# A parallel attention and feed-forward block: where small stores, statistics, splits and side work stand in the queues

## The chip, the cores and the metric

The kernel runs on one core of a Trainium2 chip. A core has five engines with a queue each: TensorE (PE in the profile; its weight loads are shown as PEld), VectorE (DVE), ScalarE (ACT), GpSimd (POOL) and SyncE (SP), which here only issues transfers. The metric is the device time of one execution in microseconds (us), as the median of several runs. An engine works through its instructions in the order in which the program wrote them; engines wait for each other, and for transfers, by semaphores.

## The reference

For x of 2048 rows and 576 columns the reference computes

```
xn  = layernorm(x)                       # no scale, no shift, eps 1e-5
out = x + A(xn) + B(xn)

A:  q, k, v = xn @ wqkv, 32 heads of 18
    for row s: 8 keys at s, s-2, ..., s-14 (masked below 0)
    softmax over the 8 logits (scale 18**-0.5), weighted sum of v, @ wo
B:  h = relu(xn @ w1 + b1) ** 2          # 4608 columns
    h @ w2 + b2
```

All inputs are float32.

## The kernel before, in words

**Precision.** TensorE multiplies in a 32-bit form of reduced precision (fp32r). So every operand is split into a high part (a copy on ACT) and a low part (a subtraction on DVE), and a product is made of several matmuls: `split`, `wq_hi`/`wq_lo`, `w1_hi`/`w1_lo`, `w2_hi`/`w2_lo`, `normalize`. A split on ACT followed by one on DVE therefore stands ahead of every group of matmuls.

**Blocks and stages.** The 2048 rows are 4 blocks (`b`) of 512, and the columns of the features are 5 tiles of 128 (the last has 64). Heads are 4 groups (`g`) of 8. The program runs through these stages:

- `open_rows`: normalises block 0 row by row and multiplies group 0 of Q, K, V. The first inverse deviation is a `pow` on GpSimd (`inverse_std`, L130).
- `q0`: 28 rows of Q, K, V products (`qkv_row`, L301 to L306; a row is 14 matmuls of 432 columns) for blocks 0 and 1, of which 26 run in its loop and two in the first pair that follows. Between the rows generators in `pieces` are advanced: `statistics(1)`, the splits of the weights of a group (`split_wq`), `normalize(1)`, the sums of blocks (`sums`).
- `phase_a(0)`: 18 pairs (`ffn_pair`) of tiles of the hidden layer for blocks 0 and 1 together, by a scheme with fewer products out of sums of blocks and of W1's parts (`combine_w1`, slots T1 to T4). Block 0's second product (`tile_products`, L494) is interleaved as `work(0..3)`; block 1's hidden tiles go to DRAM (`hscr`).
- `phase_b0`: block 1's second product, tile by tile, from the hidden tiles loaded again, with the Q, K, V rows of blocks 2 and 3 between.
- `phase_a(1)` and `phase_b1`: the same for blocks 2 and 3. In each stage the attention output of a block is regrouped (`regroup`, from DRAM by GpSimd's queue), transposed on DVE (`o_hi`) and multiplied by wo (`o_ops`) at the end.

**Attention as side work.** Attention runs on DVE (`attention`, a generator of 18 steps for a block and group: 8 for the logits, 2 for the softmax, 8 for the weighted sum). `side(k)` advances it by k steps; with `exp=False` it stops ahead of the step that holds the exponential on ACT. `run(pieces, k)` advances the pieces first and gives what is left of k to `side`. `queue` holds the groups offered so far, `loads` and `fetch` their transfers, and three buffers `kv` limit how many are loaded. `complete(b)` finishes all of a block's attention at once.

**What sets the order.** The order is written out by hand; nothing is rearranged. Rows of Q, K, V are copied from PSUM into the one tile `st` (`qkv_out`, L295) and stored two rows at a time by SP (L298), so the copy of a row into one half of `st` comes after the landing of the stores that read this half. In `q0`, `turn_mr` transposes the statistics of block 1 on TensorE, copies and stores them, and `load_mb` loads them again for all partitions; `normalize(1)` needs that load. SP's transfers are issued in the order of the program, and each load waits on SP until its buffer is free. The keys' and values' scratch has 16 rows of zeros ahead of it: 8 small stores (`scr[k][g][:PAD]`), two by SP ahead of `open_rows` and six behind it.

**In a pair** (`ffn_pair`), PSUM banks `ba`, `bb`, `bc` hold the products. DVE adds `bc` and the copy `u` (`tt(r1[:, 1], ...)`, `tt(r0[:, 1], ...)`) between two products into the same bank, so TensorE waits for these sums. The first pair of a stage (`first`) has another order at its end (`fourth` ahead of `third`).

Of the kernel before, what the change touches and what calls it, by code (L numbers as in the profile page):

```python
# [25 lines left out]
G = 4  # L26
# [5 lines left out]
PAD = 16  # L32
# [13 lines left out]
def block_kernel(ctx: ExitStack, tc: tile.TileContext, x, xt, wqkv, wo, w1, b1, w2, b2, out):  # L46
    nc = tc.nc
# [19 lines left out]
    zero = sb.tile([PAD, CG], F32, name="pr")  # L67
# [437 lines left out]
    def ffn_pair(s, p, work, first=False):  # L505
        b0, b1 = 2 * s, 2 * s + 1
        n = s * NP + p
        ba, bb, bc = (bank(i) for i in F_BANKS[s])
        f0, f1 = 2 * p, 2 * p + 1
        last = p == NP - 1  # L510
        A11 = lambda k, c: X[b0][:, k, c]
        A12 = lambda k, c: X[b0][:, k, 2 + c]
        A22 = lambda k, c: X[b1][:, k, 2 + c]
        S4 = lambda k, c: X[b1][:, k, c]
        ss = lambda i: lambda k, c: SS[i][:, k, c]

        def weight(slot, k, c):
            return w1s[n, slot // 4][:, k, slot % 4, c * P:(c + 1) * P]

        def product(to, slot, a, start=False):  # L520
            mm = [(weight(slot, 0, c), a(0, c)) for c in range(2)]
            for c in range(2):
                mm += [(weight(slot, 1, c), a(0, c)), (weight(slot, 0, c), a(1, c))]
            for i, (l, r) in enumerate(mm):
                nc.tensor.matmul(to, l, r, start=start and i == 0, stop=i == len(mm) - 1, skip_group_check=True)  # L525

        def left(to, f, v):
            for k in range(2):
                nc.tensor.matmul(to, weight(LEFT, k, f), v, start=False, stop=k == 1, skip_group_check=True)  # L529

        def relu(to, a, f):
            nc.scalar.activation(to, a, AF.Relu, bias=b1t[:, f:f + 1])  # L532

        def square_hi(r):
            h = mt.tile([P, 2, 2, TB], F32R, name="h", bufs=3)
            nc.scalar.activation(h[:, 0], r, AF.Square)  # L536
            return h

        def square(r):
            nc.scalar.activation(r, r, AF.Square)  # L540

        def square_lo(r, h):
            tt(h[:, 1], r, h[:, 0].bitcast(F32), ALU.subtract)

        def finish_pair():
            r0, r1, h0 = prev.pop("r")
            h1 = square_hi(r1)
            square_lo(r0, h0)
            square(r1)
            yield  # L550
            square_lo(r1, h1)
            nc.sync.dma_start(hscr[s][p], h1.rearrange("p k f t -> p (k f t)").bitcast(F32))
            yield

        before = prev.pop("finish", None)
        product(ba, B11, A11, start=True)
        if first:
            nc.tensor.matmul(bb, weight(B11, 0, 0), A11(0, 0), start=True, stop=True, skip_group_check=True)
        nc.scalar.activation(bb, ba, AF.Copy)
        product(bc, T1, ss(1), start=True)  # L560
        if before:
            next(before)
        if not last:
            combine_w1(n + 1)
        if not first:
            side(1, False)
        work(0)
        product(bb, T2, ss(2))
        w2_hi()
        u = four()  # L570
        nc.scalar.activation(u[:, 0], bb, AF.Copy)
        if not first:
            left(bc, 1, x4[b1])
        work(1)
        if before:
            next(before)
        w2_lo()
        if not last:
            w1_hi(n + 1, 0)
        w2_hi()  # L580
        product(bb, T3, ss(3))
        if first:
            left(bc, 1, x4[b1])
        if not last:
            w1_lo(n + 1, 0)
        w2_lo()
        nc.scalar.activation(u[:, 1], bb, AF.Copy)
        r0, r1 = four(), four()
        tt(r1[:, 1], bc, u[:, 1], ALU.add)
        if not last:  # L590
            w1_hi(n + 1, 1)
            w1_lo(n + 1, 1)
        product(ba, B21, A12)
        left(ba, 0, x4[b0])
        relu(r1[:, 1], r1[:, 1], f1)
        relu(r0[:, 0], ba, f0)
        work(2)

        def third():
            product(bc, B22, S4)  # L600
            left(bc, 1, x4["d"])
            side(2)
            tt(r0[:, 1], bc, u[:, 0], ALU.add)
            relu(r0[:, 1], r0[:, 1], f1)

        def fourth():
            product(bb, T4, A22)
            left(bb, 0, x4[b1])
            relu(r1[:, 0], bb, f0)

        if first:
            fourth()
            third()
            h0 = square_hi(r0)
        else:
            third()
            h0 = square_hi(r0)
            fourth()
        square(r0)
        side(2, False)  # L620
        work(3)
        hs[n] = h0
        prev["r"] = r0, r1, h0
        prev["finish"] = finish_pair()
# [126 lines left out]
    def phase_b0():  # L751
# [8 lines left out]
        for n in range(NF):  # L760
            w2_hi()
            add(b, tile_products(b, n, hs[0, n // 2]))
            w2_lo()
            if n % 2 and n // 2 + 3 < NP:
                load_h(0, n // 2 + 3)
            run(pieces, 2 if n < 9 else 1)
            while r < 32 and 32 * (n - 6) > 25 * r:
                bb, g, j = todo[r]
                while bb not in normed or g not in split_up:
                    run(pieces, 1)  # L770
                qkv_row(bb, g, j, 2 + r % 3)
                r += 1
                if r == 2:
                    pieces.append(split_wq(1, "w1s", lambda: load_wq(2)))
                if r == 8:
                    pieces.append(split_wq(2, "S", lambda: load_wq(3)))
                if r == 16:
                    pieces.append(split_wq(3, "w1s"))
                if r == 24:
                    pieces.append(sums(1))  # L780
                if j == NJ - 1 and bb == 2:
                    offer(2, g)
                run(pieces, 2)
            if n == 31:
                run_all(pieces)
                last_sum(1)
                complete(1)
                load_w1(NP)
                load_w1(NP + 1)
                regroup(b, 0)  # L790
                regroup(b, 1)
                for g in range(G):
                    offer(3, g)
            if n == 33:
                residual(b)
                combine_w1(NP)
            if n in (33, 34):
                c = 2 * (n - 33)
                o_hi(b, c), o_hi(b, c + 1)
                o_lo(b, c), o_lo(b, c + 1)  # L800
# [26 lines left out]
    def phase_b1():  # L827
        b = 3
        open_y(b)
        for n in range(NF - 2):  # L830
            w2_hi()
            add(b, tile_products(b, n, hs[1, n // 2]))
            w2_lo()
            if n % 2 and n // 2 + 3 < NP:
                load_h(1, n // 2 + 3)
            if n == 22:
                complete(b)
                regroup(b, 0)
                residual(b)
                residual_left(b)  # L840
            if n == 25:
                regroup(b, 1)
            if n in range(27, 27 + NC):
                o_hi(b, n - 27)
                o_lo(b, n - 27)
            side(2)
        for c in range(NC):
            w2_hi()
            add(b, o_ops(b, c), (NC - 2,) if c == NC - 1 else ())
            w2_lo()  # L850
        tail()
# [213 lines left out]
    def q0():  # L1065
# [20 lines left out]

        for r in range(len(todo) - 2):
            row(r)
            if r == 2:
                run_all(pieces)  # L1090
                turn_mr(1, 7)
                load_mb(1)
                load_wq(2)
                offer(0, 0)
                for late in held:
                    late()
                held.clear()
                pieces += [normalize(1)]
            if r == 5:
                lane[0] = nc.gpsimd  # L1100
                load_w1(0)
                pieces.insert(0, split_wq(2, "h", lambda: load_wq(0)))
# [7 lines left out]
            if r == 21:  # L1110
                run_all(pieces)
                for n in range(3):
                    load_w2(n)
            if r == 23:
                combine_w1(0)
                load_w1(1)
            if r in (24, 25):
                w1_hi(0, r - 24)
                w1_lo(0, r - 24)
            elif r != 3:  # L1120
                run(pieces, 3 if r < 2 or 15 <= r < 20 else 2)

        def filler(i):
            if i < 2:
# [4 lines left out]
        return filler  # L1129

    warm_up(WARM)
    for k in "kv":
        nc.sync.dma_start(scr[k][0][:PAD], zero)
    load_wq(1)
    load_rows(1)
    nc.sync.dma_start(b1t, b1)
    nc.sync.dma_start(b2t, b2)
    load_xt(1)
    open_rows()
    for g in range(1, G):  # L1140
        for k in "kv":
            nc.sync.dma_start(scr[k][g][:PAD], zero)
    load_wq(3)
    free[0] = 2
    filler = q0()
# [54 lines left out]
```

## Time and profile before

| | |
|---|---|
| time, median of 3 runs | 1153.28 us (1151.89 to 1153.41) |
| the profiled execution: its own time | 1151.24 us |
| its span, from the first to the last instruction | 1149.3 us |
| TensorE busy | 1122.4 us (98%) |
| VectorE busy | 914.7 us (80%) |
| ScalarE busy | 572.5 us (50%) |
| GpSimd busy | 110.9 us (10%) |
| moved by DMA | 254.25 MB, mean 221 GB/s |
| mean granted clock of TensorE | 0.993 |

How to read it: a busy TensorE is not TensorE at its peak, and the idle time of an engine that isn't the bottleneck costs nothing. Of a timeline's row the first number is the start from the beginning of the span, the second the duration; in brackets stands the idle time of that engine just before it, and what ended it. The releaser is inferred: where several semaphores are waited for, the one that came last by the profile is named. `SPq` and `POOLq` are the queues that issue transfers. A line number such as L94 can be that of a helper (L94 is every `tt`), so the tiles' names tell the operations apart. The stages lie about here: rows of `q0` from 22 to 98 us, first stage of pairs to 426, the rows with block 1's tiles from 476 to 640, second stage of pairs from 668 to 987, the last stage from 1010.

### The profile page before, as it was taken

How to read it: one execution, taken by the hardware profiler on the slowest of the kernel's cores; microseconds unless marked ns; L12 is line 12 of the kernel's file. 1: busy time of each engine (PE TensorE's matmuls, PEld its weight loads, DVE VectorE, ACT ScalarE, POOL GpSimd, SP SyncE). 2: the span in 40 equal slices, each digit the busy share in tenths (PEclk: the TensorE clock that was granted, in tenths of full speed). 3: DMA queues.
4: the chain of work that ended last, by engine and by line, in shares of the span. 5: the costliest groups of instructions: out<-in, count | busy, mean ns of one | idle time of the engine just before them, and what ended most of it. 6: DMA issues, size and time to landing. Idle time of an engine off the chain costs nothing.

```text
span 1149.3 us, 13816 instructions
## 1 busy us (share of the span) xinstructions
PE 1122.4 (98%) x5014; PEld 939.7 (82%) x5014; DVE 914.7 (80%) x1202; ACT 572.5 (50%) x801; POOL 110.9 (10%) x211
## 2 busy tenths in 40 slices
PE   9897999999999999999999989999999999999998
PEld 7896788888888888888888768888888888887777
DVE  7687898887888777888787778887978888689944
ACT  5323676666766763521222247667666676422221
POOL 3001010020020020010210100020100102001110
PEclk9998999999999999999999999999999999999999
DMA  7866545468458488978766765374552745779783
GB/s 243 280 219 209 188 156 202 155 155 251 148 165 234 155 296 290 346 265 316 258 213 236 248 221 188 107 237 160 195 206 93 261 155 191 272 262 369 268 340 99
DMA packets 89476, 254.25 MB, mean 221 GB/s; under 512 B 12472, under 2 KB 40896, under 8 KB 74816
## 3 DMA queue, kind: packets, MB, share of 16 engines
q1 hardware_dynamic: 78832, 200.94, 51.0%
q0 software_dynamic: 10288, 52.06, 13.7%
q8 instruction: 39, 0.64, 0.2%
q10 hardware_dynamic: 288, 0.37, 0.1%
q14 instruction: 29, 0.24, 0.1%
HBM read 191.90 MB, written 61.43 MB: 220 GB/s over the span
## 4 chain that ended last, share of the span: by engine, by line
PE 79%; DVE 12%; DMA 4%; issue 3%; ACT 1%; POOL 0%; DVEq 0%; ACTq 0%; POOLq 0%; SPq 0%
PE p L494 35%; PE p L525 29%; PE p L305 9%; PE p L529 5%; DVE pr L94 5%; DVE w2s L94 2%; DVE w1r L94 1%; DMA h<-in_xt 1%; DMA r<-in_wqkv 1%; DMA st<-o 1%; PE p L982 1%; DMA o<-q 1%; DVE w1s L94 1%; DVE r L94 0%; ACT w2s L467 0%
## 5 line engine op out<-in xcount | busy, mean ns | idle before, releaser
L494 PE MATMUL p<-h,w2s 128*128 128x512 f32 x2010 | 487.0, 390 | 4.8 <-ACT w2s L467 2.6
L494 PEld LDWEIGHTS p<-h,w2s 128*128 128x128 f32 x2010 | 376.2, 188 | 87.8 <-ACT w2s L467 3.9
L525 PE MATMUL p<-X,w1s 128*128 128x512 f32 x864 | 220.9, 391 | 7.9 <-ACT w1s L440 3.9
L525 PEld LDWEIGHTS p<-X,w1s 128*128 128x128 f32 x864 | 162.3, 188 | 43.4 <-ACT w1s L440 4.2
L467 ACT ACTIVATE w2s<-w2r 128x640 fp32r<-128x640 f32 x164 | 119.4, 732 | 103.4 <-PE p L494 50.3
L525 PE MATMUL p<-S,w1s 128*128 128x512 f32 x648 | 165.7, 391 | 1.8 <-DVE r L94 1.8
L94 DVE TENSOR_TENSOR w2s<-w2r,w2s 128x576 fp32r<-128x576 f32 x164 | 123.1, 754 | 55.7 <-ACT w2s L467 55.0
L525 PEld LDWEIGHTS p<-S,w1s 128*128 128x128 f32 x648 | 122.3, 189 | 28.2 <-DVE r L94 2.7
L94 DVE TENSOR_TENSOR h<-r,h 128x1024 fp32r<-128x1024 f32 (+2 forms) x78 | 93.1, 1198 | 46.6 <-ACT r L540 43.7
L382 POOL DMA_DIRECT2D o<-q x128 | 69.2, 608 | 539.2 <-DVE q L94 537.6
L94 DVE TENSOR_TENSOR w1s<-w1r,w1s 128x1024 fp32r<-128x1024 f32 x72 | 88.1, 1224 | 30.5 <-ACT w1s L440 29.8
L532 ACT ACTIVATE r<-r,b1t 128x512 f32<-128x512 f32 x72 | 51.9, 721 | 117.6 <-DVE r L94 117.6
L295 ACT ACTIVATE st<-p 128x432 f32<-128x432 f32 x64 | 33.1, 528 | 143.4 <-PE p L305 98.6
L354 DVE TENSOR_REDUCE lg<-pr 128x64 f32<-128x1152 f32 x64 | 86.5, 1351 | 1.3
L94 DVE TENSOR_TENSOR pr<-lg,kv 128x1152 f32<-128x1152 f32 x64 | 86.7, 1354 | 1.1
L94 DVE TENSOR_TENSOR pr<-q,kv 128x1152 f32<-128x1152 f32 x64 | 86.6, 1354 | 0.9
L440 ACT ACTIVATE w1s<-w1r 128x1024 fp32r<-128x1024 f32 x72 | 75.6, 1050 | 10.1 <-PE p L494 5.2
L94 DVE TENSOR_TENSOR pr<-pr 128x576 f32<-128x576 f32 (+1 forms) x128 | 77.6, 606 | 3.4
L536 ACT ACTIVATE h<-r 128x1024 fp32r<-128x1024 f32 x72 | 76.1, 1057 | 4.5 <-DMA h<-h 3.4
L540 ACT ACTIVATE r<-r 128x1024 f32<-128x1024 f32 x72 | 76.0, 1055 | 1.2
L529 PE MATMUL p<-x,w1s 128*128 128x512 f32 x216 | 66.5, 389 | 0.0
L494 PE MATMUL p<-w1s,w2s 128*128 128x512 f32 x260 | 62.3, 398 | 2.9 <-ACT w2s L467 2.7
(133 smaller groups left out, 1041.2 us busy)
## 6 DMA issues: line engine op xcount, KB each, us to landing
h<-h SPq DMA_DIRECT2D x72, 1024.0 KB, 5.4
w2r<-in_w SPq DMA_DIRECT2D x144, 320.0 KB, 4.5
w1r<-in_w SPq DMA_DIRECT2D x36, 640.0 KB, 4.2
kv<-vscr POOLq DMA_DIRECT2D x15, 1296.0 KB, 7.8
kv<-kscr POOLq DMA_DIRECT2D x14, 1296.0 KB, 7.4
r<-in_wqkv SPq DMA_DIRECT2D x16, 432.0 KB, 5.8
w2r<-in_wo SPq DMA_DIRECT2D x20, 320.0 KB, 3.8
w1r<-in_xt SPq DMA_DIRECT2D x6, 1024.0 KB, 7.0
```

Of the source, the lines that this page charges most:

```text
L94: return nc.vector.tensor_tensor(out=out, in0=a, in1=b, op=op)
L305: nc.tensor.matmul(p[:, :QW], l, r, start=k == 0, stop=k == len(mm) - 1)
L354: nc.vector.tensor_reduce(out=lg[:, j * HG:(j + 1) * HG].rearrange("p a w -> p w a"), in_=pr.rearrange("p w (a d) -> p w a d", d=DH), axis ...
L382: nc.gpsimd.dma_start(rows[:, i], q[i * L:(i + 1) * L, :, a:z])
L440: nc.scalar.activation(w1s[n, k][:, 0], raw1[n][:, 4 * k:4 * k + 4], AF.Copy)
L467: nc.scalar.activation(w2s[stream[i]][:, :DE], raw2[i], AF.Copy)
L494: nc.tensor.matmul(yp[b][c], v, a, start=c not in yb[b], stop=c in last and c not in [o[0] for o in ops[i + 1:]], skip_group_check=True)
L525: nc.tensor.matmul(to, l, r, start=start and i == 0, stop=i == len(mm) - 1, skip_group_check=True)
L529: nc.tensor.matmul(to, weight(LEFT, k, f), v, start=False, stop=k == 1, skip_group_check=True)
L532: nc.scalar.activation(to, a, AF.Relu, bias=b1t[:, f:f + 1])
L536: nc.scalar.activation(h[:, 0], r, AF.Square)
L540: nc.scalar.activation(r, r, AF.Square)
```

## The change

The diff has these parts.

- **Zeros.** All eight stores of zeros are issued on GpSimd's queue ahead of `open_rows`; SP issues none.
- **Statistics of block 1.** In `q0`, after row 1 one more piece is run (the last of `statistics(1)`), and `turn_mr` and `load_mb` follow there, ahead of pieces of the split of group 3's weights. Before, they stood after row 2, behind that split. Fewer pieces are run at row 1.
- **Group 2's split.** `split_wq(2, ...)`, `load_w1(0)` and the change of the loads to GpSimd's queue move from after row 5 to after row 6.
- **W1's first sums.** `combine_w1(0)` and `load_w1(1)` move from after row 23 to after row 21, and from row 21 on one step is run after a row instead of two.
- **First pairs.** In the first pair of each stage the splits of w2 and w1 (`splits()`) come after `tt(r1[:, 1], ...)`, and `third` has no `side(2)`. In the other pairs `splits()` stands ahead of the product T3, where most of these calls stood; the two last come ahead of that product in the program's text, but no engine's own order changes by it.
- **Side work.** In odd pairs `side(2, False)` instead of `side(1, False)` is run near the start.
- **Blocks 2 and 3.** The rows of Q, K, V are due in 22 tiles instead of 25, and what followed at tile 31 (last sums, `complete(1)`, loads of W1, `regroup`) follows at tile 28.
- **Last stage.** Block 3's regrouping follows as soon as its attention is done, at tile 22 at the latest, with both parts at once (before: at tiles 22 and 25).

```diff
--- before.py
+++ after.py
@@ -563,7 +563,7 @@
         if not last:
             combine_w1(n + 1)
         if not first:
-            side(1, False)
+            side(1 + p % 2, False)
         work(0)
         product(bb, T2, ss(2))
         w2_hi()
@@ -574,19 +574,26 @@
         work(1)
         if before:
             next(before)
-        w2_lo()
-        if not last:
-            w1_hi(n + 1, 0)
-        w2_hi()
+
+        def splits():
+            w2_lo()
+            if not last:
+                w1_hi(n + 1, 0)
+            w2_hi()
+            if not last:
+                w1_lo(n + 1, 0)
+            w2_lo()
+
+        if not first:
+            splits()
         product(bb, T3, ss(3))
         if first:
             left(bc, 1, x4[b1])
-        if not last:
-            w1_lo(n + 1, 0)
-        w2_lo()
         nc.scalar.activation(u[:, 1], bb, AF.Copy)
         r0, r1 = four(), four()
         tt(r1[:, 1], bc, u[:, 1], ALU.add)
+        if first:
+            splits()
         if not last:
             w1_hi(n + 1, 1)
             w1_lo(n + 1, 1)
@@ -599,7 +606,8 @@
         def third():
             product(bc, B22, S4)
             left(bc, 1, x4["d"])
-            side(2)
+            if not first:
+                side(2)
             tt(r0[:, 1], bc, u[:, 0], ALU.add)
             relu(r0[:, 1], r0[:, 1], f1)
 
@@ -764,7 +772,7 @@
             if n % 2 and n // 2 + 3 < NP:
                 load_h(0, n // 2 + 3)
             run(pieces, 2 if n < 9 else 1)
-            while r < 32 and 32 * (n - 6) > 25 * r:
+            while r < 32 and 32 * (n - 6) > 22 * r:
                 bb, g, j = todo[r]
                 while bb not in normed or g not in split_up:
                     run(pieces, 1)
@@ -781,7 +789,7 @@
                 if j == NJ - 1 and bb == 2:
                     offer(2, g)
                 run(pieces, 2)
-            if n == 31:
+            if n == 28:
                 run_all(pieces)
                 last_sum(1)
                 complete(1)
@@ -833,13 +841,12 @@
             w2_lo()
             if n % 2 and n // 2 + 3 < NP:
                 load_h(1, n // 2 + 3)
-            if n == 22:
+            if b not in xr and (n == 22 or not queue and current[0] is None):
                 complete(b)
                 regroup(b, 0)
+                regroup(b, 1)
                 residual(b)
                 residual_left(b)
-            if n == 25:
-                regroup(b, 1)
             if n in range(27, 27 + NC):
                 o_hi(b, n - 27)
                 o_lo(b, n - 27)
@@ -1086,17 +1093,19 @@
 
         for r in range(len(todo) - 2):
             row(r)
+            if r == 1:
+                run(pieces, 1)
+                turn_mr(1, 7)
+                load_mb(1)
             if r == 2:
                 run_all(pieces)
-                turn_mr(1, 7)
-                load_mb(1)
                 load_wq(2)
                 offer(0, 0)
                 for late in held:
                     late()
                 held.clear()
                 pieces += [normalize(1)]
-            if r == 5:
+            if r == 6:
                 lane[0] = nc.gpsimd
                 load_w1(0)
                 pieces.insert(0, split_wq(2, "h", lambda: load_wq(0)))
@@ -1111,14 +1120,13 @@
                 run_all(pieces)
                 for n in range(3):
                     load_w2(n)
-            if r == 23:
                 combine_w1(0)
                 load_w1(1)
             if r in (24, 25):
                 w1_hi(0, r - 24)
                 w1_lo(0, r - 24)
             elif r != 3:
-                run(pieces, 3 if r < 2 or 15 <= r < 20 else 2)
+                run(pieces, 3 if r < 1 or 15 <= r < 20 else 1 if r > 20 else 2)
 
         def filler(i):
             if i < 2:
@@ -1129,17 +1137,15 @@
         return filler
 
     warm_up(WARM)
-    for k in "kv":
-        nc.sync.dma_start(scr[k][0][:PAD], zero)
+    for g in range(G):
+        for k in "kv":
+            nc.gpsimd.dma_start(scr[k][g][:PAD], zero)
     load_wq(1)
     load_rows(1)
     nc.sync.dma_start(b1t, b1)
     nc.sync.dma_start(b2t, b2)
     load_xt(1)
     open_rows()
-    for g in range(1, G):
-        for k in "kv":
-            nc.sync.dma_start(scr[k][g][:PAD], zero)
     load_wq(3)
     free[0] = 2
     filler = q0()
```

## The prediction

> **What bounds the kernel now.** First read: the page (span, busy shares), then the view of waits for TensorE (who waits for whom: us in total, times, longest).
>
> ```profile
> span 1149.3 us, 13816 instructions
> PE 1122.4 (98%) x5014; PEld 939.7 (82%) x5014; DVE 914.7 (80%) x1202; ACT 572.5 (50%) x801; POOL 110.9 (10%) x211
> ...
> PE p L494 <- ACT w2s L467: 5.3, 4, 2.3
> PE p L525 <- ACT w1s L440: 3.9, 1, 3.9
> PE p L525 <- DVE r L94: 3.4, 4, 1.3
> PE p L305 <- ACT h L261: 2.6, 1, 2.6
> ```
>
> TensorE is busy for 1122.4 of 1149.3 us, and the diff adds and removes no matmul. So what can come back is the 26.9 us of idle time, a handful of single waits, and the slow matmuls that follow a long one: in the view of stretches the granted clock, third number from the end, stands at 0.50 for some 3 us after two of them.
>
> ```profile
> 49.00:50.00 1.00, 1.00 (x5) 0.91 (x4) 0.96 (x3) 0.00 (x0) 0.00 (x0) 0.50 0.96 271
> 657.00:658.00 1.00, 1.00 (x3) 0.77 (x3) 0.93 (x4) 0.00 (x0) 0.00 (x0) 0.50 0.60 69
> ```
>
> The profiled execution took 1151.24 us (its span and 1.9 us around it), 2.0 below the median of 1153.28. The sum is a difference; I set it against both. All further rows but the one marked are from timelines (start, duration, engine, line, and in brackets the idle time before with what ended it).
>
> **1. Zeros on GpSimd's queue.** Eight stores of 9 KB leave SP and stand on POOL ahead of the first `pow`.
>
> ```profile
> 1.69 0.25 POOL L71 TENSOR_SCALAR_AFFINE_SELECT mask<-mask 128x32 f32<-128x32 f32 x1
> 6.50 0.57 POOL L130 TENSOR_TENSOR rs<-rs,half 128x1 f32<-128x1 f32 x1 [4.56 <-DVE rs L129]
> 63.84 0.75 POOL L327 DMA_DIRECT2D kv<-vscr  x1 [35.36 <-DMA r<-in_wqkv]
> 99.15 4.33 POOL L382 DMA_DIRECT2D o<-q  x8 [34.56 <-DVE q L94]
> 27.08 1.37 SPq L251 DMA_DIRECT2D r<-in_wqkv  x3
> ```
>
> POOL is free at 1.94 and then idles 4.56 us. One issue like its first (0.75 us) and seven at 4.33/8 = 0.54 end at 6.5, just where the `pow` begins, and that `pow` opens the chain to row 0. Bounds: 0 (the idle time covers them; no gain, since x is loaded ahead of the zeros in both) and 1.4 (all eight at 0.75 end at 7.94). I take **+0.3**, near the lower end, where POOL's eight in a row are. SP loses six issues ahead of the load at 27.08, which comes some 2.8 us sooner; no TensorE wait hangs on it.
> [...]
>
> **2. Statistics ahead of splits.** `turn_mr`'s transpose moves from behind row 2 of Q, K, V to behind row 1, with its copy, its store and the load of mb.
>
> ```profile
> 27.39 2.52 PE L305 MATMUL p<-w1s,X 128*128 128x432 f32 x12
> 27.93 0.55 POOL L130 TENSOR_TENSOR mr<-mr,half 128x1 f32<-128x1 f32 x1 [0.67 <-DVE mr L129]
> 33.61 0.25 ACT L165 ACTIVATE mrt<-p 8x128 f32<-8x128 f32 x1
> 35.15 4.26 DMA mb<-mr
> 45.72 2.18 ACT L261 ACTIVATE h<-r 128x864 fp32r<-128x864 f32 x3
> 51.67 0.53 ACT L295 ACTIVATE st<-p 128x432 f32<-128x432 f32 x1 [3.77 <-PE p L305]
> ACT st L295 <- DMA qscr<-st: 12.6, 3, 7.0
> 46.69 0.66 PE L305 MATMUL p<-h,X 128*128 128x432 f32 x2 [2.57 <-ACT h L261]
> 51.71 2.61 PE L305 MATMUL p<-h,X 128*128 128x432 f32 x12
> ```
>
> (Rows 4 and 7 are from the chain and from ACT's waits.) Row 1 ends at 27.4, the last `pow` at 28.5: TensorE waits 1.1 us (0 to 1.2). In return the copy `mrt`, which ended at 33.9 behind the splits of S, ends near 29. SP issues row 1's stores (copy 0.53, three issues of 0.46) until 29.5, then mr, which needed 1.3 us to mb's issue and now lands behind those stores: mb is issued near 31.4 and, 4.3 us later, normalising starts at 35.7 instead of 39.4.
> Behind normalising stood the split of group 2's weights, h, for which row 8 waited. But this split is now inserted after row 6, not row 5. So on ACT it comes behind row 6's copy into `st`, and that copy may not overwrite its half of `st` until row 3's stores have landed: ACT's waits name these stores with up to 7.0 us, and the copy at 51.67 is row 6's. (The bracket names a matmul, but row 6's had long ended.) The stores queue behind wq, q, k and v, which SP issues after mb; they landed 12.2 us after mb (39.4 to 51.6), so now at 47.9. Copy 0.5, first split 0.9: row 8 starts near 49.5, after a gap of 4.3 us. Before, with its half clock, it took from 46.69 to 51.71; I give it 4.8. Row 9 starts at **54.3, 2.6 us later** than before. Bounds: 47.9 (a row of 2.7 us directly behind row 7, 3.8 earlier) and 55.7 (the stores land 1.4 later).
>
> **3. W1's first sums ahead.** The end of the rows, and DVE there:
>
> ```profile
> 98.03 0.55 PE L305 MATMUL p<-h,x 128*128 128x432 f32 x2
> 107.90 2.49 PE L525 MATMUL p<-S,w1s 128*128 128x512 f32 x6
> 110.23 2.52 PE L305 MATMUL p<-h,X 128*128 128x432 f32 x12
> 104.33 2.35 DVE L94 TENSOR_TENSOR w1s<-w1r,w1s 128x1024 fp32r<-128x1024 f32 x2
> L354 DVE TENSOR_REDUCE lg<-pr 128x64 f32<-128x1152 f32 x64 | 86.5, 1351 | 1.3
> ```
>
> (The last row is a group of the page: 1351 ns is the mean of one attention step.) Rows end at 98.6; the first pair's 13 matmuls, 3.0 us at 0.23 each (12.99/56, row at 1111.41 in part 6), end at 110.2: 8.6 us are lost. The three sums move ahead, and three attention steps (4.1 us) fall out ahead of the first split w1s, which ended at 105.5. DVE's start on attention stays where it is, since the late ACT holds DVE's splits of h too; so this split ends at 101.4. The rows now end at 98.6 + 2.6 = 101.2. Hardly a wait is left, and no half clock: the products end at 101.2 + 0.2 + 3.0 = 104.4, so parts 2 and 3 together are **-5.8**. Bounds: -3 (a wait of 3 us stays) and -12 (row 8 on time as well). `load_w1(1)` moves past two rows of stores on SP; its buffer is free by then: 0.
>
> **4. First pairs reordered.** Only where `first`: the splits follow `tt(r1)`, and two attention steps leave `third`.
>
> ```profile
> 127.73 1.65 PE L525 MATMUL p<-S,w1s 128*128 128x512 f32 x6 [0.92 <-DVE r L94]
> 684.67 1.66 PE L525 MATMUL p<-X,w1s 128*128 128x512 f32 x6 [1.27 <-DVE r L94]
> 689.06 1.65 PE L525 MATMUL p<-S,w1s 128*128 128x512 f32 x6 [0.92 <-DVE r L94]
> ```
>
> The four waits for r are 3.4 us; with the shorter idle times and the slower matmuls behind them I count 2.6 us start to start in the first stage and 3.3 in the second. r1 goes ahead of some 3 us of splits, r0 loses 2.7 us of steps. Late next is `square_hi` on ACT, some 0.5 in all: **-2.3 and -2.5** (bounds 0 to -2.6 and 0 to -3.3). In the other pairs `splits()` leaves every engine's order as it was: 0.
>
> **5. Q, K, V of blocks 2 and 3 in 22 tiles instead of 25.** Block 1's attention output is regrouped at tile 28 instead of 31.
>
> ```profile
> 653.00 1.31 DVE L692 STREAM_TRANSPOSE r<-st 128x512 f32<-128x512 f32 x2 [3.77 <-DMA st<-o]
> 655.65 8.26 PE L494 MATMUL p<-w1s,w2s 128*128 128x512 f32 x28 [2.15 <-ACT w2s L467]
> 668.27 1.53 PE L525 MATMUL p<-X,w1s 128*128 128x512 f32 x6
> ```
>
> DVE's transposes waited 3.77 us for the regrouped tile, and ACT's split of w2s stood behind them. With three tiles (14 matmuls, 3.2 us each) more, the load is covered. From 655.65 to 668.27 stand 42 matmuls, 9.7 us' worth; with the 2.15 ahead, 5.1 us are lost. I leave 1.1 for DVE's chain of transposes, late next: **-4.0** (bounds -2 and -5.1). Rows come 14% denser in tiles, but each tile's share of TensorE grows with them; if DVE or the loads of weights fall behind, up to +3; I take 0, as no wait stands between 475 and 653.
> [...]
>
> **6. One more attention step in odd pairs, block 3 closed early.**
>
> ```profile
> 346.64 1.23 DVE L94 TENSOR_TENSOR w1s<-w1r,w1s 128x1024 fp32r<-128x1024 f32 x1 [0.71 <-ACT w1s L440]
> 349.09 0.69 DVE L94 TENSOR_TENSOR r<-p,r 128x512 f32<-128x512 f32 x1 [0.46 <-ACT r L587]
> 351.66 1.52 PE L525 MATMUL p<-X,w1s 128*128 128x512 f32 x6
> ...
> 1014.56 0.41 DVE L360 TENSOR_REDUCE mx<-lg 128x32 f32<-128x256 f32 x1
> 1109.36 0.71 DVE L692 STREAM_TRANSPOSE r<-st 128x512 f32<-128x512 f32 x1 [4.62 <-DMA st<-o]
> 1056.64 52.51 PE L494 MATMUL p<-h,w2s 128*128 128x512 f32 x224 [1.49 <-DMA h<-h]
> 1111.41 12.99 PE L494 MATMUL p<-h,w2s 128*128 128x512 f32 x56 [2.27 <-ACT w2s L467]
> ```
>
> A step of 1.4 us comes ahead of both quoted DVE rows; DVE idles 0.71 + 0.46 there, so r1 ends some 0.2 later, at 350.0, and TensorE overwrites its bank at 351.66. Cost 0. Eighteen steps more, less three in the rows and four in the first pairs, are about ten fewer in the last stage, which at `mx` (1014.56) has 46 left (10 + 18 + 18) at two a tile. So block 3 ends near tile 18 and is regrouped two or three tiles ahead of tile 22, 6 to 10 us where 4.62 were short. That returns the 2.6 at 1111.41 (wait and slow start) and, of the wait at 1056.64 and the small ones behind it, about 1: **-3.5** (bounds -1, if the loads that now come together hold h, and -5.5).
>
> **Sum.** 0.3 - 5.8 - 2.3 - 2.5 - 4.0 - 3.5 = -17.8: the execution's 1151.2 becomes 1133.4, the median **1135** (1135.5).
>
> **Rivals.**
> (a) Row 8 starts on time: if row 3's stores land before 44, parts 2 and 3 give -12, total 1129. For it: mb lands 3.7 us sooner; against it: the same bytes stand ahead of the stores.
> (b) Only the rows and first pairs gain: the ends of blocks 1 and 3 stay bound by landing, since the earlier loads meet others (DMA share 0.96 in the row at 49). Parts 5 and 6 give -1 or nothing: 1142 to 1146.
> (c) Slower: the odd pairs. If the extra step pushes r1 past TensorE's next product, each of 18 pairs pays. It decides from 17.8/18 = 1.0 us a pair; a whole step of 1.4 costs 25 us: 1160. Against it: 1.66 us of slack in the quoted pair; for it: DVE already stands at 80%.
> (d) It does not do what it says: the zeros, the wait behind row 1 and the late row 8 eat what w1's sums give, and DVE's steps are only moved: 1151 to 1156.
>
> **Chances.** Forecast (1130 to 1140) 0.48; (a) 0.12; (b) 0.21; (c) 0.11; (d) 0.08. A measurement of this kernel tells about 0.2% (2.3 us) from no change. Faster: 0.48 + 0.12 + 0.21 + 0.01 of (d) = 0.82; same 0.05; slower 0.11 + 0.02 = 0.13. The range reaches from (a), 1128, over (b) to 1151, and leaves out (c) and most of (d).
>
> **What would show it.** A gap near 1.1 us behind row 1; mb landing near 36; row 8 held by ACT until about 49.5, half clock behind it; the rows' end near 101 with no long wait for w1s; no wait for r in first pairs; none near 2 us at the first output products of blocks 1 and 3. It is wrong if POOL's first `pow` starts past 7.5, if waits for r appear in odd pairs, or if transposes still wait for st<-o.

## The result

The changed kernel takes 1139.48 us (median of 4 runs, 1138.27 to 1142.67); the kernel before, measured beside it, 1152.81. The ratio is 0.9889 (95% interval 0.9868 to 0.9911), a gain of 13.3 us where 17.8 were forecast. The profiled execution took 1139.25 us.

Its page and the view of waits for TensorE (us in total, times, longest):

```profile
span 1137.5 us, 13818 instructions
PE 1117.7 (98%) x5014; PEld 937.1 (82%) x5014; DVE 912.6 (80%) x1202; ACT 575.1 (51%) x801; POOL 115.1 (10%) x219
...
PE p L494 <- ACT w2s L467: 4.7, 5, 2.2
PE p L305 <- ACT h L261: 4.3, 1, 4.3
...
PE p L525 <- DVE r L94: 1.6, 2, 0.9
PE p L494 <- DMA h<-h: 1.4, 1, 1.4
PE p L163 <- POOL mr L130: 1.0, 1, 1.0
```

The waits for w1s (3.9 and 2.4) are gone and those for r are halved. The waits for w2s are nearly what they were (4.7 after 5.3), and the one of row 8 for its weights h (ACT's split, L261) has grown from 2.6 to 4.3. Where they lie, in TensorE's timeline:

```profile
28.22 0.27 PE L163 MATMUL p<-mb,mr 128*8 128x128 f32 x1 [0.98 <-POOL mr L130]
49.28 4.29 PE L305 MATMUL p<-h,X 128*128 128x432 f32 x12 [4.34 <-ACT h L261]
...
100.41 1.55 PE L525 MATMUL p<-X,w1s 128*128 128x512 f32 x6
...
103.41 2.51 PE L305 MATMUL p<-h,X 128*128 128x432 f32 x12
...
131.08 1.65 PE L525 MATMUL p<-X,w1s 128*128 128x512 f32 x6 [0.64 <-DVE r L94]
...
647.51 3.49 PE L494 MATMUL p<-w1s,w2s 128*128 128x512 f32 x14 [2.23 <-ACT w2s L467]
652.07 4.75 PE L494 MATMUL p<-w1s,w2s 128*128 128x512 f32 x18 [1.07 <-ACT w2s L467]
...
659.38 1.52 PE L525 MATMUL p<-X,w1s 128*128 128x512 f32 x6
...
690.34 1.65 PE L525 MATMUL p<-X,w1s 128*128 128x512 f32 x6 [0.92 <-DVE r L94]
...
1042.81 30.00 PE L494 MATMUL p<-h,w2s 128*128 128x512 f32 x126 [0.70 <-ACT w2s L467]
1074.25 38.39 PE L494 MATMUL p<-h,w2s 128*128 128x512 f32 x168 [1.45 <-DMA h<-h]
```

Both kernels issue the same 5014 matmuls, so the start of each can be set against its twin. The difference is -0.3 us after the opening and -6.8 at the end of the first pair's first products (103.41 against 110.23). The first pair brings it to -9.2 and pair 1 back to -8.3; the end of block 1 adds only 0.6 (-8.9: 659.38 against 668.27). The second stage's first pair brings it to -11.6, its pair 1 back to -10.4, and the last stage to -11.8, the difference of the spans. So the rows and the first pairs gave a little more than was forecast (11.9 against 10.3), the ends of blocks 1 and 3 gave 2.0 of 7.5, and pair 1 of the two stages took 2.2 back.

### The profile page after: what moved, and what is told of

It reads as the page before. It is cut to its first block, busy times and chain, and to the rows that moved or that the text cites. A ratio compares the mean times of both kernels' runs of the same rounds, so it can differ in the third digit from the quotient of the medians.

```text
span 1137.5 us, 13818 instructions
## 1 busy us (share of the span) xinstructions
PE 1117.7 (98%) x5014; PEld 937.1 (82%) x5014; DVE 912.6 (80%) x1202; ACT 575.1 (51%) x801; POOL 115.1 (10%) x219
## 4 chain that ended last, share of the span: by engine, by line
PE 83%; DVE 7%; DMA 5%; issue 2%; ACT 1%; SPq 1%; POOL 1%; ACTq 0%; DVEq 0%; POOLq 0%
PE p L494 35%; PE p L525 29%; PE p L305 13%; PE p L529 5%; DMA w2r<-in_w 2%; DVE w2s L94 2%; DVE pr L94 1%; PE p L989 1%; DMA h<-h 1%; DMA qscr<-st 1%; DVE w1s L94 1%; DVE lg L354 1%; DMA q<-qscr 1%; DVE w1r L94 0%; DVE h L94 0%
```

## The experiments

Each is the changed kernel (1139.48) with one edit (e10_row5_no_steps has two, e11_all five). The kernel before took 1151.7 to 1152.9 in the sessions of these runs, so medians that lie about 1 us apart are not told apart by this table. All medians:

| run | time, us | ratio to before, 95% |
|---|---|---|
| the changed kernel | 1139.48 | 0.9868 to 0.9911 |
| e1_row5 | 1136.93 | 0.9845 to 0.9875 |
| e2_third | 1143.51 | 0.9902 to 0.9939 |
| e3_q0_before | 1143.22 | 0.9896 to 0.9930 |
| e4_zero_sp | 1143.03 | 0.9892 to 0.9929 |
| e5_w1_late | 1138.67 | 0.9844 to 0.9915 |
| e6_w1_early | 1135.88 | 0.9811 to 0.9887 |
| e7_step_p3 | 1136.81 | 0.9828 to 0.9893 |
| e8_resid_late | 1138.63 | 0.9845 to 0.9909 |
| e9_first_order | 1144.58 | 0.9914 to 0.9961 |
| e10_row5_no_steps | 1134.29 | 0.9822 to 0.9857 |
| e11_all | 1126.44 | 0.9756 to 0.9790 |
| e12_one_step | 1150.12 | 0.9957 to 0.9983 |

### Zeros on SP again

```diff
+    for k in "kv":
+        nc.sync.dma_start(scr[k][0][:PAD], zero)
-    for g in range(G):
-        for k in "kv":
-            nc.gpsimd.dma_start(scr[k][g][:PAD], zero)
     load_wq(1)
...
     open_rows()
+    for g in range(1, G):
+        for k in "kv":
+            nc.sync.dma_start(scr[k][g][:PAD], zero)
     load_wq(3)
```

> Part 1 undone: the zeros go by SP again, two ahead of the second weights' load and six ahead of the load of group 3. Prediction's term: +0.3 by the queue move, so without it -0.3: 1139.2. The trace of the changed kernel speaks for the other sign (first power of -0.5 at 6.04 instead of 6.50, opening 0.33 earlier): then 1139.8. If the later loads of weights, six issues of about 0.46 us later on SP, hold the split of a group, up to 1142.

It cost 3.6 us, more than any of the three expected. In the chain of waits of this run (start, us, what) and in TensorE's timeline:

```profile
29.87 4.74 DMA mr<-mrt
...
53.01 5.06 PE L305 MATMUL p<-h,X 128*128 128x432 f32 x12 [8.03 <-ACT h L261]
```

The statistics are stored (mr) at 29.87, nearly as early as in the changed kernel (29.42). But with six issues more ahead of it, SP issued the load of group 3's weights only at 26.83 to 27.82 (23.91 to 24.99 in the changed kernel), and that load and row 1's stores land first, at 32.93 and 34.41: the store takes 4.74 us where it took 1.22 before the change. The load of mb follows 4.8 us behind it, not 1.7 as in the changed kernel, and row 8 waits 8.03 us.

### Parts 2 and 3 undone

```diff
-            if r == 1:
-                run(pieces, 1)
-                turn_mr(1, 7)
-                load_mb(1)
             if r == 2:
                 run_all(pieces)
+                turn_mr(1, 7)
+                load_mb(1)
...
-            if r == 6:
+            if r == 5:
...
+            if r == 23:
                 combine_w1(0)
                 load_w1(1)
...
-                run(pieces, 3 if r < 1 or 15 <= r < 20 else 1 if r > 20 else 2)
+                run(pieces, 3 if r < 2 or 15 <= r < 20 else 2)
```

> Parts 2 and 3 undone: statistics behind row 2, the split after row 5, W1's first sums after row 23, the run counts as before; all else is the changed kernel. Theory: the first stage's product ends near 110 again, 6.5 us later than in the changed kernel (103.4), and nothing later gives it back: 1146 (1145 to 1147). Rival: the later stages are bound by loads that are issued at their own time and give a part of it back: 1142 to 1144.

The time is the rival's, but not for the rival's reason: nothing is given back later. The first pair's products already end sooner than 110. The row behind these products, of this run and then of the run with zeros on SP:

```profile
107.18 2.50 PE L305 MATMUL p<-h,X 128*128 128x432 f32 x12
```

```profile
108.60 2.51 PE L305 MATMUL p<-h,X 128*128 128x432 f32 x12
```

So parts 1 to 3 make four cases: neither 110.23, zeros alone 107.18 (-3.1), statistics and sums alone 108.60 (-1.6), both 103.41 (-6.8). Each is worth more with the other, because both serve one chain: group 3's load, row 1's stores, mr, mb, normalising, group 2's split, row 8.

### The split after row 5, and a third staging buffer

```diff
-            if r == 6:
+            if r == 5:
                 lane[0] = nc.gpsimd
                 load_w1(0)
                 pieces.insert(0, split_wq(2, "h", lambda: load_wq(0)))
```

> The split of group 2's weights, with the first W1 load and the change of lanes, is inserted after row 5 again instead of row 6; everything else is the changed kernel. Theory: on ACT the split then stands ahead of row 6's copy into st, so it no longer waits for row 3's stores (5.65 us in the changed kernel). Row 8 starts about 45.0 instead of 49.28, its half clock goes, and of the 6 us between the mean pace and row 9's start 4 to 6 come back: about 1134.5 (1133 to 1136), against 1139.5 of the changed kernel. Rival: the split waits for normalising X or for group 2's own load anyway; then row 8 still starts past 48 and the time stays within 1 us of 1139.5.

In the other run the split stays after row 6, and rows 4 and 5 are staged in the tile `pr`, which attention uses later:

```diff
+        if n == 8:
+            stage[1] = sb.tile([P, 2, QW], F32, name="pr")
+        i = (n // 2 + (9 < n < 100)) % 2
+        st = stage[1] if n in (8, 9) else stage[0][:, 2 * i:2 * i + 2]
...
-        nc.scalar.activation(stage[0][:, j], p[:, :QW], AF.Copy)
+        nc.scalar.activation(st[:, j % 2], p[:, :QW], AF.Copy)
```

> Rows 4 and 5 of Q, K and V are staged in a third buffer (the idle tile pr), so that row 6's copy goes to the half that rows 0 and 1 left and need not wait for row 3's stores; the split stays behind row 6. Theory that the landing of row 3's stores, and not the order on ACT alone, holds row 8: row 6's copy runs near 43.5, row 8 starts about 45.5, and the time is that of the run with the split after row 5, within 1 us (about 1135). Rival: it is the order on ACT (the copy comes late whatever buffer it fills, because ACT is busy with X until about 45): row 8 starts past 48, and the time stays within 1 us of 1139.5.

In ACT's timeline, first of the changed kernel, then of the run with the third buffer:

```profile
47.88 0.53 ACT L295 ACTIVATE st<-p 128x432 f32<-128x432 f32 x1 [5.65 <-DMA qscr<-st]
48.31 2.18 ACT L261 ACTIVATE h<-r 128x864 fp32r<-128x864 f32 x3
```

```profile
42.55 0.52 ACT L302 ACTIVATE st<-p 128x432 f32<-128x432 f32 x1
42.97 2.19 ACT L261 ACTIVATE h<-r 128x864 fp32r<-128x864 f32 x3
```

Row 6's copy came 5.3 us sooner and row 8 started at 44.95, with the split after row 5 at 44.71. So it is the landing of row 3's stores that holds row 8 in the changed kernel. But neither run kept the gain. The run with the split after row 5 was 6.4 us ahead of the changed kernel from row 9 on and lost 4.1 of it at the end of the rows (TensorE's and DVE's timelines):

```profile
97.14 2.08 PE L525 MATMUL p<-X,w1s 128*128 128x512 f32 x4 [2.47 <-DVE w1s L94]
...
95.65 0.31 DVE L94 TENSOR_TENSOR q<-pr 128x144 f32<-128x144 f32 x1
95.87 2.35 DVE L94 TENSOR_TENSOR w1s<-w1r,w1s 128x1024 fp32r<-128x1024 f32 x2
```

DVE finishes an attention step (`q`) at 95.9 and only then splits w1s. In the run with the third buffer attention itself began late, since it needs `pr` back from the stores of rows 4 and 5:

```profile
58.28 1.36 DVE L94 TENSOR_TENSOR pr<-q,kv 128x1152 f32<-128x1152 f32 x1 [9.96 <-DMA qscr<-pr]
```

It began at 53.69 in the changed kernel; here w1s came so late that TensorE waited 4.29 us for it. Of this run only the part at row 8 says something; its time is that of a badly chosen buffer.

### No attention steps behind the last rows

```diff
-            if r == 6:
+            if r == 5:
...
-                run(pieces, 3 if r < 1 or 15 <= r < 20 else 1 if r > 20 else 2)
+                run(pieces, 3 if r < 1 or 15 <= r < 20 else 0 if r > 20 else 2)
```

> The split after row 5, as in the first run, and no attention step behind rows 21 to 23 (one each in the changed kernel), so that DVE reaches the split of w1s three steps sooner (4.1 us at 1.36). Theory: with row 8 on time the end of the rows is bound by DVE, which stands in attention steps until 95.9 and lets TensorE wait 2.47 us at 97.14; without them this wait and the half clock behind it go, and 3 us more come back than by the first run: 1134 (1133 to 1135) against 1136.9 there. Rival: the split waits for ACT or for the load of W1 instead: 1136 to 1137.

As expected, 2.6 us less than with the split alone. No wait over 0.5 us is left between row 1 and pair 1, and the row behind the first pair's products starts at 96.88, 6.5 us ahead of the changed kernel.

### W1's loads at block 1's end, later and earlier

```diff
             if n == 28:
...
-                load_w1(NP)
-                load_w1(NP + 1)
                 regroup(b, 0)
                 regroup(b, 1)
                 for g in range(G):
                     offer(3, g)
+            if n == 31:
+                load_w1(NP)
+                load_w1(NP + 1)
```

> The two loads of W1 (640 KB together), which stand on SP ahead of w2r and h at tile 28 of block 1, are issued at tile 31 instead. Theory for the failed term of Q, K, V: the wait before block 1's output products is the landing of w2r (issued 628.49, landed 640.53 in the changed kernel), because the load meets W1, h, q, k, v and the regrouped tile; without W1 ahead, w2r lands some 2 to 3 us sooner, ACT's split of w2s moves ahead by as much, and the two waits of 2.23 and 1.07 shrink to 1 or less: about 1137 (1136 to 1138) against 1139.5. Rival: the regrouped tile (landing 643.95) or DVE's transposes of it are late next, at the same time as w2r: then less than 0.7 us comes back.

In the other run the two calls stand under `if n == 23:` instead.

> The same two loads of W1 are issued at tile 23 of block 1, some 20 us ahead, where the queue has room (their tiles are free from 594.5). Same theory: w2r lands 2 to 3 us sooner and 2 to 3 us come back, 1137 (1136 to 1138); then it is the bytes ahead in the queue and not the place of W1. Rival: DVE's transposes are late next and less than 0.7 us comes back. If it gains and the late one does not, the late one pays in W1's own landing ahead of the pairs.

First the changed kernel: the issue of w2r on SP, the DMA share (last but one number) of a stretch after it, and ACT's split that waits for it.

```profile
628.49 0.33 SPq L457 DMA_DIRECT2D w2r<-in_w  x1
...
635.00:640.00 5.00, 5.00 (x24) 4.14 (x23) 0.79 (x1) 0.00 (x0) 0.00 (x0) 1.00 1.00 416
...
640.63 0.74 ACT L467 ACTIVATE w2s<-w2r 128x640 fp32r<-128x640 f32 x1 [6.90 <-DMA w2r<-in_w]
```

320 KB took 12.0 us (landed at 640.53), with a mean DMA share of 1.02 over that time: two loads of W1, h, q and k of the next group and the regrouped tile were all asked for within 6 us. With W1 loaded late, ACT's split came at 637.47, 3.2 us sooner, as the theory had it, and yet TensorE waited 1.39 and 1.08. DVE's timeline of that run says why:

```profile
642.98 1.61 DVE L94 TENSOR_TENSOR w1r<-w1r 128x512 f32<-128x512 f32 x3 [2.71 <-DMA w1r<-in_w]
644.51 1.30 DVE L700 STREAM_TRANSPOSE r<-st 128x512 f32<-128x512 f32 x2
```

W1's sums stand ahead of the transposes on DVE, and now they wait for W1. Only 0.8 us came back, close to the rival: DVE's transposes are late, but for W1 and not for the regrouped tile. With W1 loaded early neither is late: the waits for w2s fall to 1.0 in all, and 3.6 us come back; set against the changed kernel matmul by matmul, 3.5 of them at this place.

### The additional step only from pair 3 on

```diff
-            side(1 + p % 2, False)
+            side(1 + (p % 2 if p > 1 else 0), False)
```

> The additional attention step is left out in pair 1 of each stage and stays in the odd pairs from 3 on. Theory: the step costs only in pair 1, where r stands late already (waits of 0.64 and 0.92 before its second product); 0.9 and 1.05 us come back, less what two attention steps more in block 3 cost (2.8 us of DVE, not on the path): about 1137.8 (1137 to 1138.5). Rival: pair 1 waits for r whatever the step (the first pair leaves DVE late): within 0.5 us of 1139.5.

Both waits for r in pair 1 are gone; in the first stage:

```profile
131.21 1.52 PE L525 MATMUL p<-X,w1s 128*128 128x512 f32 x6
```

No other pair waits for r in either kernel. So the additional step costs nothing from pair 3 on, and about 1 us in each pair 1. The trace gains 1.0 and 1.2 us at these places. At the wait for h near 1074, which this run doesn't have, it gains 1.5 more. Of these 3.7 us the span keeps 2.5 (1135.0 after 1137.5); the mean granted clock is 0.995, not 0.998.

### Block 3's residual later

```diff
-            if b not in xr and (n == 22 or not queue and current[0] is None):
+            if b not in [k for k, _ in ob] and (n == 22 or not queue and current[0] is None):
                 complete(b)
                 regroup(b, 0)
                 regroup(b, 1)
+            if n == 29:
                 residual(b)
                 residual_left(b)
```

> Block 3's residual, with its load of x into w1r (1 MB), is issued at tile 29 instead of together with the regrouping of the attention output near tile 18. Theory for the failed term of closing block 3 early: the wait of 1.45 at 1074.25 is the landing of h (issued 1062.80, landed 1074.12), which queues behind that load; without it h lands some 4 us sooner, the wait goes and about 1.5 us come back: 1138 (1137.5 to 1138.5). Rival: the output's end then waits for the residual (it is needed at the last products): 1140 or more; or the regrouped tiles alone fill the queues and h lands no sooner than 1073: within 0.5 of 1139.5.

0.9 us less, and the wait for h is gone. This does not settle it: the wait is absent too in the runs with W1 late and with the step from pair 3, where the residual is loaded as in the changed kernel. There h landed within 1 us of its need. What the load itself costs stays open.

### First pairs as before

```diff
-        if not first:
-            splits()
+        splits()
         product(bb, T3, ss(3))
...
-        if first:
-            splits()
...
-            if not first:
-                side(2)
+            side(2)
```

> Part 4 undone: in the first pair of each stage the splits stand ahead of the product T3 and the two attention steps in the third place again. Theory (terms -2.3 and -2.5, read in the traces as -2.4 and -3.1): the waits for r of 0.9 to 1.3 us come back in both first pairs and the time is 1144.5 (1143.5 to 1145.5) against 1139.5. Rival: pair 1 now waits for r in the changed kernel (0.64 and 0.92) because the work was only moved there; with the old order these waits go and about 2 us less is lost: 1142 to 1143.

5.1 us more, as by the traces: 2.4 us in the first stage and 2.7 in the second (the 3.1 of the expectation takes in some of block 1's end). The waits for r are six then (4.8 us); pair 1 still has its two (0.62 and 0.90), so these were not moved there by the new order.

### One attention step in every pair

```diff
-            side(1 + p % 2, False)
+            side(1, False)
```

> Part 6's first half undone: one attention step in every pair, as before, all else as in the changed kernel. Theory: the two waits for r in pair 1 go (-1.9), and 18 steps more stand in block 3's stage, so that its output is regrouped at tile 22 again; the wait for h at 1074.25 goes (-1.5) and the wait of 2.3 near 1100 for the regrouped output comes back with its slow matmuls (+2.6): 1138.7 (1137.5 to 1140), so the additional step was worth nothing as it stands. Rival: the step is worth what the prediction said (-3.5 with block 3 closed early), only hidden by pair 1: then 1141 or more.

Far off: 10.6 us more, beyond the rival too. The waits for r in pair 1 are gone, as expected (2.2 us by the trace). But 5.1 us are lost at block 1's end: h, issued at 627.00 as in the changed kernel (626.99), lands at 641.89 and not at 636.91. Here q, k and v of an attention group are asked for just ahead of it (621.35 to 623.40); that they hold it up is not shown by a run of its own. And 9.7 us are lost here, in TensorE's and DVE's timelines of this run:

```profile
1092.86 30.79 PE L494 MATMUL p<-h,w2s 128*128 128x512 f32 x122 [6.14 <-DVE w2s L94]
...
1076.34 0.41 DVE L360 TENSOR_REDUCE mx<-lg 128x32 f32<-128x256 f32 x1
...
1091.82 0.31 DVE L94 TENSOR_TENSOR q<-pr 128x144 f32<-128x144 f32 x1
```

DVE's last softmax stands at 1076.34, as it did before the change:

```profile
1076.08 0.41 DVE L360 TENSOR_REDUCE mx<-lg 128x32 f32<-128x256 f32 x1
```

But TensorE reaches tile 22 some 7 us sooner than it did then (the last matmul ahead of the wait starts at 1086.10, its twin before the change at 1093.23). There `complete(3)` runs what is left of attention at once, ahead of DVE's split of w2s.

### All that gained, together

The five edits shown above in one kernel: split after row 5, no steps behind rows 21 to 23, W1 at tile 23, the step from pair 3 on, the residual at tile 29.

```diff
-            if r == 6:
+            if r == 5:
...
-                run(pieces, 3 if r < 1 or 15 <= r < 20 else 1 if r > 20 else 2)
+                run(pieces, 3 if r < 1 or 15 <= r < 20 else 0 if r > 20 else 2)
...
+            if n == 23:
+                load_w1(NP)
+                load_w1(NP + 1)
...
-            side(1 + p % 2, False)
+            side(1 + (p % 2 if p > 1 else 0), False)
...
-            if b not in xr and (n == 22 or not queue and current[0] is None):
+            if b not in [k for k, _ in ob] and (n == 22 or not queue and current[0] is None):
...
+            if n == 29:
                 residual(b)
                 residual_left(b)
```

> All that gained, together: split after row 5, no attention steps behind rows 21 to 23, W1 of the second stage loaded at tile 23, the additional step from pair 3 on, block 3's residual at tile 29. Theory that the places are independent: -5.5 (rows), -2.4 (W1), -1.5 (pair 1, less the steps that move to the end) and -1 (residual) from 1139.5: 1129 (1127.5 to 1131). Rival: the gains overlap, because an earlier start of a stage only moves the loads' clump under TensorE: 1132 or more.

1126.44 us, 13.0 below the changed kernel (1.1%), better than the sum expected and its range:

```profile
span 1125.8 us, 13814 instructions
PE 1114.5 (99%) x5014; PEld 936.1 (83%) x5014; DVE 911.7 (81%) x1202; ACT 574.4 (51%) x801; POOL 117.6 (10%) x219
...
PE p L494 <- ACT w2s L467: 1.5, 4, 0.5
PE p L494 <- DMA h<-h: 1.1, 1, 1.1
```

Set against the changed kernel matmul by matmul, the rows, pair 1 and block 1's end give all of it. The last stage gives nothing (-12.1 at its start and at its end), so the late residual isn't shown to gain here either.

## Why the prediction was partly right

The time came 4.5 us above the forecast and half a us inside its range of 1130 to 1140, and the sign was right. That it lies inside is in part luck. By the two traces parts 5 and 6 gave nothing in sum (-0.6, +2.2 and -1.4), which is rival (b), priced at 1142 to 1146; the rows and first pairs gave 1.6 us more than forecast. One of the prediction's own signs of being wrong is there, waits for r in an odd pair (pair 1), and the wait near 2 us at block 1's first output products, which was to be gone, is there too. By its terms:

| term | forecast | by the two traces | undone, by medians |
|---|---|---|---|
| 1 zeros | +0.3 | -3.1 alone | +3.6 |
| 2, 3 statistics, sums | -5.8 | -1.6 alone; with 1 -6.8 | +3.7 |
| 4 first pairs | -2.3, -2.5 | -2.4, -2.7 | +5.1 |
| 5 rows in 22 tiles | -4.0 | -0.6 | not tried alone |
| 6 step, block 3 | -3.5 | +2.2 (pair 1), -1.4 (last stage) | +10.6 (the step) |

**Term 1 failed, and its error was hidden in terms 2 and 3.** GpSimd's side was right: the first `pow` came at 6.04 and the opening got no longer. The step that failed is the sentence that the load at 27.08 comes 2.8 us sooner and "no TensorE wait hangs on it". Row 8's wait for h hung on it, at the end of a chain through SP's order. The opening was 0.3 us shorter where 0.3 more was forecast, but this settles nothing: in the traces with the zeros on GpSimd the first row behind it starts anywhere from 21.37 to 22.18, and with them on SP at 21.63 and 21.92.

**Terms 2 and 3 had the right times for the wrong cause.** Forecast were mb's issue near 31.4, the stores' landing at 47.9, row 8 at 49.5, the rows' end at 101.2 and the products' at 104.4; they came at 31.13, 47.41, 49.28, 100.4 and 103.41. But the step that takes the earlier load of mb as the gain of moving the statistics needs the zeros gone: without that mb is issued at 34.66, 0.5 us sooner than before, while with the zeros gone and the statistics where they were it is issued at 32.22, 2.9 sooner. The sum of the three terms (-5.5 forecast, -6.8 measured) was near because the shift was counted once. Two smaller readings were off: half clock follows three waits and not two before the change (for 6.8 us from 103.09), and row 9 came 2.1 us later and not 2.6, as row 8 took 4.5 us and not 4.8.

**Term 4 was right** in place and size.

**Term 5 failed at** "With three tiles more, the load is covered". The regrouping came earlier, as said, but the loads asked for at the same tile came earlier with it and met. The waits grew a little (2.23 and 1.07 after 2.15 and 0.57), and what held them up changed from the regrouped tile to w2r. The 0.6 us that did come are owed to the granted clock, which stood at 0.50 behind the wait before the change (656.05 to 659.46) and at 1.00 behind this one; no run shows that the change brought this about (see the last section). This is rival (b), which had named the collision. The early load of W1 brought 3.5 us more at this place, so about the forecast 4.0 were to be had there.

**Term 6 failed in two steps.** "Cost 0" was read from a pair in the middle (346); it holds for all odd pairs but the first of each stage, where the step costs 1.0 and 1.2 us (why DVE has less slack there is not shown). That is rival (c) at 2 of 18 places. And at the last stage the 2.6 us at 1111.41 did come back, but new waits of 0.70 and 1.45 took 1.2 of them. Yet without the step the changed kernel loses 10.6 us, not 3.5: the prediction asked what the additional steps give on top of the other parts, but not what these parts cost without them. By the trace of that run, DVE's last softmax stands where it stood before the change, while TensorE arrives 7 us sooner: the seven steps taken out of the rows and the first pairs, and what TensorE gained, had to be made up by DVE.

**Rival (a)**, row 8 on time, was priced at -12 for parts 2 and 3. The experiment gave 2.6 of the further 6: DVE, not row 8, then bounds the end of the rows. With three steps less on DVE all of it was kept (6.5 by the trace, 5.2 by the medians).

## What to carry to other kernels

Small stores that nobody waits for, back on SP, put the load issued behind six of them 2.8 us later (its last issue at 27.82 after 24.99), and the run took 3.6 us more; follow the queue down to the next load that someone does wait for before such a store is costed at nothing. Undo each part by itself before crediting it. Parts that serve one chain can be worth more together than apart (-3.1 and -1.6 alone, -6.8 together), and where side work on one engine (here attention on DVE) has to keep pace with another, the part that looked like -3.5 carried 10.6. If work is brought forward, its loads come along: spread them into the stretch ahead, where the DMA share was low (0.33 and 0.39 between 590 and 600 in the changed kernel), not behind, where the next consumer stands.

## What was not expected of the hardware

After nearly equal waits TensorE's granted clock (third number from the end) fell or did not. The changed kernel after the wait of 2.23 at 647.51:

```profile
649.00:650.00 1.00, 1.00 (x6) 0.81 (x5) 1.00 (x2) 0.00 (x0) 0.00 (x0) 1.00 1.02 425
```

The run with zeros on SP, after a shorter wait of 1.81 at 651.96:

```profile
655.00:656.00 1.00, 1.00 (x4) 0.71 (x4) 0.89 (x3) 1.00 (x3) 0.00 (x0) 0.50 0.74 292
```

Before the change 2.15 us led to 0.50 (656.05 to 659.46). So the slow matmuls that the prediction counted with such a wait do not follow from its length alone. Single waits of TensorE and the granted clock in the 4 us behind them:

| trace | wait of TensorE, us | lowest granted clock behind it |
|---|---|---|
| before | 2.15 to 655.65 | 0.50 |
| before | 2.27 to 1111.41 | 1.00 |
| changed | 2.23 to 647.51 | 1.00 |
| changed | 1.45 to 1074.25 | 1.00 |
| zeros on SP | 1.81 to 651.96 | 0.50 |
| split after row 5 | 2.44 to 645.44 | 0.50 |
| third staging buffer | 2.60 to 653.78 | 0.50 |
| split after row 5, no steps | 1.93 to 1087.27 | 1.00 |

A wait of 1.81 us was followed by half clock, and waits of 1.93, 2.23 and 2.27 were not. What else decides is not shown. So the full clock behind the changed kernel's wait of 2.23 us is what one trace shows, and no part of the change is credited with it.
